# Product accumulators as one-bank PSUM tiles from pools closed and reopened inside one plan, in an attention and channel-mix kernel

## The chip, the cores and the metric

The kernel runs on one core of a Trainium2 chip. The metric is the device time of one execution in microseconds (us), from three runs. The profile comes from one further execution of the same program.

## What is computed

Sigmoid attention over 8 batches of 12 heads (448 tokens, head size 64), then a channel mix with two weight products and a gate. All is float32 to the outside.

```python
scores = q @ k.T / sqrt(64) - log(448)
attn   = sigmoid(scores) @ v                 # heads side by side: x is (8, 448, 768)
x_prev = x shifted by one token
xk, xr = mu_k * x + (1 - mu_k) * x_prev, mu_r * x + (1 - mu_r) * x_prev
k      = relu(xk @ w_k)                      # 768 -> 1024
r      = sigmoid(xr @ w_r)                   # 768 -> 768
out    = r * ((k * k) @ w_v)                 # 1024 -> 768
```

## The kernel before

**Engines.** PE does matmuls, ACT and DVE copy, cast, add and apply functions, SP issues every DMA. Each engine runs its own instructions strictly in the order in which they were recorded, and waits at each for what that one needs.

**Attention.** Two heads at a time (24 pairs), PE makes scores (L337, L346) into a PSUM tile `sc`, ACT applies the sigmoid from it (L361), PE weighs the values (L368, L376) into `av`, and `gather` (L386 to L390) reads `av` and stores xr and xk to DRAM. PSUM has eight banks: the ring `sc` is three tiles of two banks each, the ring `av` two tiles of one bank.

**Products.** Then come three stages: R (r), K (k) and V (out). Tokens are taken in four pairs of 448-token tiles; a 2x2 block product is made with seven multiplications p, in the order 0, 1, 5, 4, 6, 2, 3. One such multiplication is called a step here. A step has three rows of outputs (four in K), and `multiply` makes one row as one accumulation in one bank, L565: 9 matmuls (12 in V), since each operand is split into a high and a low part (cast by ACT, L501; remainder by DVE, L502) and three of the four partial products are made. The operands' buffers are a ring of eight (`rr0` to `rr5`, `qh`/`ql` twice).

Each row i has two accumulators. `xb[i]` takes steps 0 and 1, then 4, then 2; `yb[i]` gets a copy of `xb[i]` after step 0 (L601, ACT), then takes 5, 6 and 3. In the kernel before these are halves of the attention's tiles: `xb` is `sc0` first half, `sc0` second half, `sc1` first half, `av0`; `yb` is `sc1` second half, `sc2` first half, `sc2` second half, `av1`. So each row has banks of its own, but two banks of one `sc` tile belong to different rows. After other steps `evacuate` and `finish` read an accumulator out: with ACT (L581, L587, L605, L607) or with DVE (L609, L612, L595). `prime` (L552) writes each `yb` bank once with one matmul before the products.

**What sets the order.** Every operation is recorded in a `Plan` with an engine, a cost, a due time and keys that it reads and writes; keys are per bank (`("sc", i, h)`). The plan plays this through with its own costs and then emits the instructions in the order of their starts. The semaphores are put in behind that, by the framework that the tiles come from, from each tile's earlier writers and readers in the order of emission. The plan's keys don't reach it.

Of the kernel before, what the change touches and what calls it, by code (L numbers as in the profile page):

```python
# [8 lines left out]
F32 = mybir.dt.float32  # L9
F32R = mybir.dt.float32r  # L10
AF = mybir.ActivationFunctionType
ALU = mybir.AluOpType
U32 = mybir.dt.uint32
PSUM = bass.MemoryType.PSUM
# [8 lines left out]
class Plan:  # L23
# [8 lines left out]
    def op(self, engine, cost, prio, run, reads, writes, dma=None):  # L32
        i = len(self.ops)
        deps = set()
        for r in reads:
            if r in self.writer:
                deps.add(self.writer[r])
        for w in writes:
            if w in self.writer:
                deps.add(self.writer[w])  # L40
            deps.update(self.readers.get(w, ()))
        for r in reads:
            self.readers.setdefault(r, []).append(i)
        for w in writes:
            self.writer[w] = i
            self.readers[w] = []
        deps.discard(i)
        self.ops.append(Op(engine, cost, prio, run, deps, dma))
# [50 lines left out]
def attention_then_channel_mix(  # L99
# [15 lines left out]
    nc = tc.nc  # L115
    P = 128
    N, _, S = q.shape
# [5 lines left out]
    T = S  # L123
# [5 lines left out]
    NJH, NFH = NJ // 2, NF // 2  # L129
# [30 lines left out]
    def ring(pool, name, bufs, shape, dtype):  # L160
        return [pool.tile(shape, dtype, name=f"{name}{i}") for i in range(bufs)]

    def gap(pool, name, size):
        pool.tile([P, size // 4], F32, name=name)

    base = ctx.enter_context(tc.tile_pool(name="base", bufs=1, side="left"))
    apool = ctx.enter_context(tc.tile_pool(name="apool", bufs=1, side="right"))
    psum = ctx.enter_context(tc.tile_pool(name="psum", bufs=1, space=PSUM))

    slots = ring(base, "slot", 7, [P, 2 * WO], F32R)  # L170
    gap(base, "gap0", 64)
# [20 lines left out]
    mk = ring(apool, "mk", 2, [P, S], F32)  # L192
    mr = ring(apool, "mr", 2, [P, S], F32)
    gap(apool, "gap4", 128)
    sc = ring(psum, "sc", 3, [P, 2, 512], F32)
    av = ring(psum, "av", 2, [P, 512], F32)

    plan = Plan()
    op = plan.op
    SP, PE, ACT, DVE = "SP", "PE", "ACT", "DVE"  # L200
    SWITCH = 92

    def mm(n, cols=S):
        return n * max(cols / 2.4 + 2.5, 200)

    def act(n, sbuf=False, ptr=False):
        return 100 + 0.834 * n + 42 * sbuf + 93 * ptr

    def dve(n, fast=False, ptr=False):
        return 135 + n / (1.92 if fast else 0.96) + 61 * ptr  # L210
# [7 lines left out]
    def dma(dst, src, prio, reads, writes):  # L218
        ns = dst.shape[0] * math.prod(dst.shape[1:]) * 4 / 300
        op(SP, 500, prio, lambda: nc.sync.dma_start(dst, src), reads, writes, dma=ns)  # L220
# [94 lines left out]
    half = [slice(h * D, (h + 1) * D) for h in range(2)]  # L315
# [104 lines left out]
    for n in range(0, N, 2):  # L420
        at = n + 1
# [5 lines left out]
        at = n + 2  # L427
# [30 lines left out]
    e = N % RAW  # L458
# [12 lines left out]
    def take(n):  # L471
        return [late.pop() for _ in range(n)]

    cc, u2, rt_, p4 = take(3), take(4), take(3), take(4)
    ys += take(5 * NFH - len(ys))
    banks = [(sc[i][:, h, :T], ("sc", i, h)) for i in range(3) for h in range(2)]
    spare_banks = [(b[:, :T], ("av", i)) for i, b in enumerate(av)]
    xb, yb = banks[:3] + spare_banks[:1], banks[3:] + spare_banks[1:]

    SOURCE = {R_: xr_d, K_: xk_d, V_: k2_d}  # L480
    PAIRS = [(2 * s, 2 * s + 1) for s in range(NT // 2)]
# [1 line left out]
    def tokens(tile_):  # L483
        return slice(tile_ * T, (tile_ + 1) * T)
# [11 lines left out]
    def operand(stage, s, p, role, t, at):  # L496
        y, Y = y_of(stage, role, t)
        hi, lo, H, L = rr[nr[0] % len(rr)]
        nr[0] += 1
        used.setdefault((stage, s, p), []).append((hi, lo, H, L))  # L500
        op(ACT, act(T, True), at, lambda: nc.scalar.copy(hi, y), [Y], [H])  # L501
        op(DVE, dve(T), at, lambda: nc.vector.tensor_sub(lo, y, hi), [Y, H], [L])  # L502


    def right(stage, s, p, at):
        for t in range(KT[stage]):
# [16 lines left out]
            elif p == 3:  # L523
                minus(stage, 2, 1, 2, t, at)
                operand(stage, s, p, 2, t, at)

    hold.append(("x", R_, NJ - 1, B - 2))
    right(R_, 0, 0, N - 4)
    OFF = N + 2
# [17 lines left out]
    def slot_keys(g):  # L547
        return [("slot", g, h) + x for h in range(3) for x in ((), ("lo",))]

    def prime(i, at):  # L550
        hi, _, H, _ = used[R_, 0, 0][0]
        op(PE, mm(1, T), at, lambda: nc.tensor.matmul(yb[i][0], slots[0][:, :P], hi, start=True, stop=True, skip_group_check=True), [H] + slot_keys(0), [yb[i][1]])  # L552

    def multiply(stage, s, p, i, at):
        g = POS[p]
        bank, K = (yb if p in (5, 6, 3) else xb)[i]
        rs_ = used[stage, s, p]
        w = CW[stage]

        def go():  # L560
            n = len(rs_)
            for t, (rh, rl, _, _) in enumerate(rs_):
                hi, lo = (slots[g][:, a * n * w + t * w + i * P:a * n * w + t * w + (i + 1) * P] for a in range(2))
                for e, (a, b) in enumerate(((hi, rh), (hi, rl), (lo, rh))):
                    nc.tensor.matmul(bank, a, b, start=p in (0, 4) and (t, e) == (0, 0), stop=(t, e) == (n - 1, 2), skip_group_check=True)  # L565

        op(PE, mm(3 * len(rs_), T), at, go, [k for r in rs_ for k in r[2:]] + slot_keys(g), [K])


    def finish(stage, s, half, par, i, src, R, c, at):  # L570
        if c is None:
            u = ncc[0] % len(cc)
            ncc[0] += 1
            c, C = cc[u]
        else:
            C = R[0]
        rows = KT[R_] if stage != K_ else NFH
        m, tile_ = half * rows + i, PAIRS[s][par]
        cols = tokens(tile_)
        if stage == R_:  # L580
            op(ACT, act(T, src is c), at, lambda: nc.scalar.activation(c, src, AF.Sigmoid), R, [C])  # L581
            dma(r_d[m][:, cols], c, at, [C], [("r", m, tile_)])
        elif stage == K_:
            if src is c and half == 0:
                op(DVE, dve(T), at, lambda: nc.vector.scalar_tensor_tensor(c, src, 0.0, src, ALU.max, ALU.mult), R, [C])  # L585
            else:
                op(ACT, act(T, src is c), at, lambda: nc.scalar.activation(c, src, AF.Relu), R, [C])  # L587
                op(ACT, act(T, True), at, lambda: nc.scalar.activation(c, c, AF.Square), [C], [C])
            dma(k2_d[m][:, cols], c, at, [C], [("x", V_, m, tile_)])
        else:  # L590
            v_ = nrt[0] % len(rt_)
            nrt[0] += 1
            r, G = rt_[v_]
            dma(r, r_d[m][:, cols], at - 1.5, [("r", m, tile_)], [G])
            op(DVE, dve(T), at, lambda: nc.vector.tensor_mul(c, src, r), R + [G], [C])  # L595
            dma(out[m * P:(m + 1) * P, cols], c, at, [C], [])

    def evacuate(stage, s, p, i, at):
        (x, X), (y, Y), (u, U), (f, F) = (z[i] for z in (xb, yb, u2, p4))
        if p == 0:  # L600
            op(ACT, act(T), at, lambda: nc.scalar.copy(y, x), [X], [Y])  # L601
        elif p == 1:
            finish(stage, s, 0, 0, i, x, [X], None, at)
        elif p == 5:
            op(ACT, act(T), at, lambda: nc.scalar.copy(u, y), [Y], [U])  # L605
        elif p == 4:
            op(ACT, act(T), at, lambda: nc.scalar.copy(f, x), [X], [F])  # L607
        elif p == 6:
            op(DVE, dve(T), at, lambda: nc.vector.tensor_add(f, y, f), [Y, F], [F])  # L609
            finish(stage, s, 1, 1, i, f, [F], f, at)  # L610
        elif p == 2:
            op(DVE, dve(T), at, lambda: nc.vector.tensor_add(u, x, u), [X, U], [U])  # L612
            finish(stage, s, 0, 1, i, u, [U], u, at)
        elif p == 3:
            finish(stage, s, 1, 0, i, y, [Y], None, at)

# [4 lines left out]
    for stage, w, out7, pace in ((K_, w_k, wk_o, WK_PACE), (V_, w_v, wv_o, WV_PACE)):  # L621
        at = OFF + first[stage - 1]
        for t in range(WK_EARLY * (stage == K_), KT[stage]):
            convert_seven(w, t, KT[stage], CW[stage], pace, at, to_dram(out7, t, CW[stage]))
            at += 4 * pace
    for i in range(4):
        prime(i, OFF - 0.1 if i < NJH else OFF + 6)
    for step, (stage, s, p) in enumerate(steps):
        at = OFF + step
        if (stage, s, p) not in used:  # L630
            right(stage, s, p, at + PREP)
        rows = NFH if stage == K_ else NJH
        for i in range(rows):
            multiply(stage, s, p, i, at + i / rows)
            evacuate(stage, s, p, i, at + i / rows + EVAC)
        if stage < V_ and last[stage, p] == step:
            load_weight(stage + 1, p, OFF + max(step + 1.5, first[stage + 1] - 8 + POS[p]))
# [42 lines left out]
```

## Time and profile before

| | |
|---|---|
| three runs | 834.77, 835.23, 835.48 us, median 835.23 |
| the profiled execution | 834.95 us, of which the span of its instructions is 833.2 |
| attention on PE | about 4 to 259 us |
| stage R / K / V on PE | from about 259, 415 and 624 us |
| DMA | 179.69 MB, 216 GB/s over the span |

In rows of the timeline and of the chain the first number is the start in us from the span's start, the second the time to the end of the group, then the engine, the line, the operation, output<-inputs and the count. "[0.66 <-ACT sc L601]" means that the engine had been idle for 0.66 us just before, until that ACT instruction ended. PEld is the weight load of PE, SPq the queue of SP. A matmul of 448 columns is shown from its start to its modelled end, and the next one starts before that end.

### The profile page before, as it was taken

The numbers are of one execution on the slowest core, as the hardware profiler recorded it, in microseconds if no ns is written. First come the engines' busy times: TensorE is split into PE (matmuls) and PEld (weight loads), VectorE is DVE, ScalarE is ACT, GpSimd is POOL, SyncE is SP. The second block draws the span as 40 slices with busy tenths as digits, with TensorE's granted clock in tenths as the row PEclk, the third lists the DMA queues.
The fourth block names the chain that finished last, engine by engine and source line by source line (L and its number), as shares of the span: only waits on it lengthen the run. The fifth ranks groups of instructions, "written<-read, shape, count | busy, mean of one in ns | idle before, by whom it ended". The sixth has DMA issues, their size and how long they took to land.

```text
span 833.2 us, 13460 instructions
## 1 busy us (share of the span) xinstructions
PE 815.4 (98%) x4594; PEld 644.8 (77%) x4594; DVE 615.9 (74%) x1160; ACT 486.9 (58%) x857; POOL 0.3 (0%) x6
## 2 busy tenths in 40 slices
PE   8999999999999999999999999999999999999998
PEld 4444444544446989898989899898988989989897
DVE  3888888888898898888997727347487585776754
ACT  6787877777765545556676555555864434334341
POOL 0000000000000000000000000000000000000000
PEclk9999999999999999999999999999999999999999
DMA  7878788799986968576887542523674647555425
GB/s 230 258 258 258 241 260 264 250 300 302 318 282 230 336 223 283 190 249 228 304 263 260 165 142 112 155 89 125 222 226 143 188 155 233 158 185 175 134 67 165
DMA packets 104756, 179.69 MB, mean 216 GB/s; under 512 B 11888, under 2 KB 93296, under 8 KB 104688
## 3 DMA queue, kind: packets, MB, share of 16 engines
q1 hardware_dynamic: 104688, 178.83, 65.7%
q8 instruction: 36, 0.59, 0.3%
q14 instruction: 32, 0.26, 0.1%
HBM read 109.06 MB, written 69.73 MB: 215 GB/s over the span
## 4 chain that ended last, share of the span: by engine, by line
PE 96%; DVE 2%; ACT 1%; issue 1%; DMA 0%; DVEq 0%; SPq 0%; ACTq 0%
PE sc L565 60%; PE av L368 14%; PE sc L337 12%; PE av L565 5%; PE av L376 3%; PE sc L346 2%; ACT sc L601 1%; DVE pf L585 1%; DVE pf L612 1%; DMA qn<-in_q 0%; DVE rr L502 0%; ACT pt L587 0%; DVE slot L545 0%; ACT slot L544 0%; PE sc L552 0%
## 5 line engine op out<-in xcount | busy, mean ns | idle before, releaser
L565 PE MATMUL sc<-rr,slot 128*128 128x448 f32 x1890 | 402.8, 363 | 8.0 <-ACT sc L601 6.3
L565 PEld LDWEIGHTS sc<-rr,slot 128*128 128x128 f32 x1890 | 353.2, 187 | 36.7 <-ACT sc L601 10.0
L361 ACT ACTIVATE pf<-sc 128x896 f32<-128x896 f32 x144 | 122.7, 933 | 41.1 <-PE sc L337 41.1
L565 PE MATMUL sc<-qh,slot 128*128 128x448 f32 x420 | 138.2, 363 | 1.7 <-ACT sc L601 1.3
L368 PE MATMUL av<-pf,vn 128*64 128x448 f32 x576 | 118.6, 547 | 0.0
L565 PEld LDWEIGHTS sc<-qh,slot 128*128 128x128 f32 x420 | 78.7, 187 | 7.7 <-ACT sc L601 2.0
L368 PEld LDWEIGHTS av<-pf,vn 128*64 128x64 f32 x576 | 37.1, 136 | 59.4 <-issue 53.7
L565 PE MATMUL sc<-ql,slot 128*128 128x448 f32 x210 | 76.0, 362 | 0.0
L501 ACT CAST rr<-ys 128x448 fp32r<-128x448 f32 x66 | 36.3, 566 | 41.0 <-PE sc L565 31.8
L337 PE MATMUL sc<-qh,kh 64*128 64x448 f32 x282 | 56.8, 399 | 0.0
L337 PEld LDWEIGHTS sc<-qh,kh 64*128 64x128 f32 x282 | 26.3, 183 | 36.5 <-ACT xx L386 15.5
L337 PE MATMUL sc<-ql,kh 64*128 64x448 f32 x282 | 51.5, 362 | 0.0
L337 PE MATMUL sc<-qh,kl 64*128 64x448 f32 x282 | 51.1, 359 | 0.0
L502 DVE TENSOR_TENSOR rr<-ys,rr 128x448 fp32r<-128x448 f32 x66 | 39.0, 618 | 14.9 <-ACT rr L501 14.8
L605 ACT COPY pf<-sc 128x448 f32<-128x448 f32 x36 | 18.9, 532 | 42.1 <-PE sc L565 32.1
L313 DVE TENSOR_TENSOR kl<-kn,kh 128x384 fp32r<-128x384 f32 x47 | 26.0, 554 | 21.7 <-ACT kh L213 21.6
L565 PE MATMUL av<-rr,slot 128*128 128x448 f32 x186 | 41.8, 362 | 0.0
L565 PEld LDWEIGHTS sc<-ql,slot 128*128 128x128 f32 x210 | 39.4, 188 | 2.9
L609 DVE TENSOR_TENSOR pf<-sc,pf 128x448 f32<-128x448 f32 x24 | 15.0, 624 | 35.4 <-PE sc L565 25.8
L502 DVE TENSOR_TENSOR rr<-pf,rr 128x448 fp32r<-128x448 f32 x38 | 22.7, 620 | 24.5 <-ACT rr L501 24.4
L387 DVE TENSOR_TENSOR dx<-xx 128x448 f32<-128x448 f32 x48 | 29.9, 622 | 12.5 <-ACT xx L386 12.3
L502 DVE TENSOR_TENSOR rr<-vn,rr 128x448 fp32r<-128x448 f32 x50 | 29.6, 619 | 12.2 <-ACT rr L501 12.2
(113 smaller groups left out, 1062.4 us busy)
## 6 DMA issues: line engine op xcount, KB each, us to landing
kn<-in_k SPq DMA_DIRECT2D x48, 224.0 KB, 4.8
qn<-in_q SPq DMA_DIRECT2D x48, 224.0 KB, 5.2
vn<-in_v SPq DMA_DIRECT2D x48, 224.0 KB, 3.0
xr_d<-mr SPq DMA_DIRECT2D x48, 224.0 KB, 5.5
xk_d<-mk SPq DMA_DIRECT2D x48, 224.0 KB, 5.3
pf<-r_d SPq DMA_DIRECT2D x48, 224.0 KB, 3.3
k_d<-pf SPq DMA_DIRECT2D x34, 224.0 KB, 2.0
r_d<-pf SPq DMA_DIRECT2D x28, 224.0 KB, 2.4
```

Of the source, the lines that this page charges most:

```text
L313: op(DVE, dve(w), at, lambda src=src, hi=hi, lo=lo: nc.vector.tensor_sub(lo[i], src, hi[i]), R + [(a + "h", i)], [(a + "l", i)])
L337: nc.tensor.matmul(sc[u][:, h, :S], kk[half[h], c * P:(c + 1) * P], qq[half[h], :], start=e == 0, stop=e == len(pairs) - 1)
L346: nc.tensor.matmul(sc[u][half[h ^ (m % 2)], m % 2, :S], kn[m % RAW][half[h], KW:], qn[m % RAW][half[h], :], start=True, stop=True)
L361: op(ACT, 923, at, lambda: nc.scalar.activation(f, sc[u][:, :, :S], AF.Sigmoid, bias=NEG_LOG_S, scale=SCALE), R, K)
L368: nc.tensor.matmul(av[n % 2][half[h], :S], vn[n % 5][:, h * NC + c, :], pf[i][:, h, :], start=c == 0, stop=False)
L376: nc.tensor.matmul(av[m % 2][half[r ^ (m % 2)], :S], vn[m % 5][half[r], 2 * NC, :], pt[n // 2 % PTB][half[r], m % 2, :], start=False, stop ...
L387: op(DVE, dve(S), at, lambda: nc.vector.tensor_sub(d, x[:, 1:], x[:, :S]), [X], [G])
L501: op(ACT, act(T, True), at, lambda: nc.scalar.copy(hi, y), [Y], [H])
L502: op(DVE, dve(T), at, lambda: nc.vector.tensor_sub(lo, y, hi), [Y, H], [L])
L565: nc.tensor.matmul(bank, a, b, start=p in (0, 4) and (t, e) == (0, 0), stop=(t, e) == (n - 1, 2), skip_group_check=True)
L605: op(ACT, act(T), at, lambda: nc.scalar.copy(u, y), [Y], [U])
L609: op(DVE, dve(T), at, lambda: nc.vector.tensor_add(f, y, f), [Y, F], [F])
```

## The change

The banks of the products become eight tiles of one bank each. The attention's PSUM tiles come from two pools now, `pav` and `pscore`, and two new plan operations close a pool and open another in its place while the plan is emitted: `pscore` becomes `pb` (`xb[:3]` and `yb[:3]`) before the first product, and `pav` becomes `pb4` (`xb[3]` and `yb[3]`, used in K alone) at step 3 of all steps. Such an operation runs on no engine; its keys order it behind the last readers of the old tiles and ahead of the first writers of the new ones. As tiles exist only from then on, the products look theirs up when they are emitted (`b[0]`, `src()`, `x()`, `y()`). The fourth `prime` moves with the second pool: its due time was six steps after the first product (`OFF + 6`), and is five after it (`at + 2` at step 3). The banks are as many as before, and the operations are the same.

```diff
-    psum = ctx.enter_context(tc.tile_pool(name="psum", bufs=1, space=PSUM))
+    psa, psc = ExitStack(), ExitStack()
+    pav = psa.enter_context(tc.tile_pool(name="pav", bufs=1, space=PSUM))
+    pscore = psc.enter_context(tc.tile_pool(name="pscore", bufs=1, space=PSUM, side="right"))
...
-    sc = ring(psum, "sc", 3, [P, 2, 512], F32)
-    av = ring(psum, "av", 2, [P, 512], F32)
+    sc = ring(pscore, "sc", 3, [P, 2, 512], F32)
+    av = ring(pav, "av", 2, [P, 512], F32)
...
-    banks = [(sc[i][:, h, :T], ("sc", i, h)) for i in range(3) for h in range(2)]
-    spare_banks = [(b[:, :T], ("av", i)) for i, b in enumerate(av)]
-    xb, yb = banks[:3] + spare_banks[:1], banks[3:] + spare_banks[1:]
+    xb, yb = ([[None, (a, i)] for i in range(4)] for a in ("xb", "yb"))
+
+
+    def reopen(old, name, side, banks, after):
+        def go():
+            old.close()
+            pool = ctx.enter_context(tc.tile_pool(name=name, bufs=1, space=PSUM, side=side))
+            for i, b in enumerate(banks):
+                b[0] = pool.tile([P, 512], F32, name=f"{name}{i}")[:, :T]
+
+        op("-", 0, 0, go, [], after + [b[1] for b in banks])
...
+    reopen(psc, "pb", "right", xb[:3] + yb[:3], [("sc", u, h) for u in range(3) for h in range(2)])
     hold.append(("x", R_, NJ - 1, B - 2))
...
-                for e, (a, b) in enumerate(((hi, rh), (hi, rl), (lo, rh))):
-                    nc.tensor.matmul(bank, a, b, start=p in (0, 4) and (t, e) == (0, 0), stop=(t, e) == (n - 1, 2), skip_group_check=True)
+                for e, (l, r) in enumerate(((hi, rh), (hi, rl), (lo, rh))):
+                    nc.tensor.matmul(b[0], l, r, start=p in (0, 4) and (t, e) == (0, 0), stop=(t, e) == (n - 1, 2), skip_group_check=True)
...
-            op(ACT, act(T), at, lambda: nc.scalar.copy(y, x), [X], [Y])
+            op(ACT, act(T), at, lambda: nc.scalar.copy(y(), x()), [X], [Y])
...
-    for i in range(4):
-        prime(i, OFF - 0.1 if i < NJH else OFF + 6)
+    for i in range(3):
+        prime(i, OFF - 0.1)
     for step, (stage, s, p) in enumerate(steps):
...
+        if step == 3:
+            reopen(psa, "pb4", "left", xb[3:] + yb[3:], [("av", i) for i in range(2)])
+            prime(3, at + 2)
```

In the order of instructions, names carry the tile's number, the line numbers of the change are up to 16 higher (L565 is L576, L601 is L614, L552 is L563, L501 and L502 are L511 and L512), and brackets name the semaphores that an instruction waits for: Activation_49 is ACT's, PE_49 PE's own count, DVE_49 DVE's.

First place, PE in step 0 of the first pair: the second row of outputs, the third row, and the first matmul of step 1. Before:

```order
L565 MATMUL sc0_184<-rr0_122,slot0_114 128x448 x3
L565 MATMUL sc0_184<-rr1_123,slot0_114 128x448 x3
L565 MATMUL sc0_184<-rr2_124,slot0_114 128x448 x3
L565 MATMUL sc1_185<-rr0_122,slot0_114 128x448 [waits Activation_49]
L565 MATMUL sc1_185<-rr0_122,slot0_114 128x448 x2
L565 MATMUL sc1_185<-rr1_123,slot0_114 128x448 x3
L565 MATMUL sc1_185<-rr2_124,slot0_114 128x448 x3
L565 MATMUL sc0_184<-rr3_125,slot1_115 128x448 [waits Activation_49]
```

The same stretch after the change:

```order
L576 MATMUL pb1_2526<-rr0_125,slot0_117 128x448 x3
L576 MATMUL pb1_2526<-rr1_126,slot0_117 128x448 x3
L576 MATMUL pb1_2526<-rr2_127,slot0_117 128x448 x3
L576 MATMUL pb2_2527<-rr0_125,slot0_117 128x448 x3
L576 MATMUL pb2_2527<-rr1_126,slot0_117 128x448 x3
L576 MATMUL pb2_2527<-rr2_127,slot0_117 128x448 x3
L576 MATMUL pb0_2525<-rr3_128,slot1_118 128x448 [waits Activation_49]
```

The third row of step 0 waited for ACT at its first matmul and waits for nothing now; the first row of step 1 waits in both.

Second place, ACT from the copies of step 0 on. Before:

```order
L601 COPY sc1_185<-sc0_184 128x448 [waits PE_49,Activation_49]
L501 CAST qh0_155<-kn1_142 128x448 [waits DVE_49]
L601 COPY sc2_186<-sc0_184 128x448 [waits Activation_49]
L501 CAST qh1_156<-qn1_152 128x448 [waits DVE_49]
L601 COPY sc2_186<-sc1_185 128x448 [waits PE_49,Activation_49]
L501 CAST rr1_123<-ys0_128 128x448
```

After:

```order
L614 COPY pb3_2528<-pb0_2525 128x448 [waits PE_49,Activation_49]
L511 CAST qh0_158<-kn1_145 128x448 [waits DVE_49]
L614 COPY pb4_2529<-pb1_2526 128x448 [waits PE_49]
L511 CAST qh1_159<-qn1_155 128x448 [waits DVE_49]
L614 COPY pb5_2530<-pb2_2527 128x448 [waits PE_49]
L511 CAST rr0_125<-vn3_151 128x448 [waits DVE_49]
```

Before, one wait for PE stood ahead of the first two copies, and each copy has a wait for PE of its own now; the cast of the third operand of step 5 (`rr0<-vn`) has moved up, to right behind the copies.

Third place, PE around the fourth prime. Before, it stood behind step 1 (slot1), and the first row of step 4 (slot3) came ahead of step 5 (slot2):

```order
L565 MATMUL sc1_185<-rr5_127,slot1_115 128x448 x3
L552 MATMUL av1_188<-rr0_122,slot0_114 128x448
L565 MATMUL sc0_184<-rr1_123,slot3_117 128x448 [waits Activation_49]
L565 MATMUL sc0_184<-rr1_123,slot3_117 128x448 [waits DVE_49]
L565 MATMUL sc0_184<-rr1_123,slot3_117 128x448
```

After, it stands between step 6 (slot4) and step 2 (slot5):

```order
L576 MATMUL pb5_2530<-qh0_158,slot4_121 128x448
L563 MATMUL pb41_2565<-rr0_125,slot0_117 128x448 [waits PE_49]
L576 MATMUL pb0_2525<-qh1_159,slot5_122 128x448 [waits Activation_49]
L576 MATMUL pb0_2525<-ql1_161,slot5_122 128x448 [waits DVE_49]
L576 MATMUL pb0_2525<-qh1_159,slot5_122 128x448
L576 MATMUL pb0_2525<-rr0_125,slot5_122 128x448 [waits Activation_49]
L576 MATMUL pb0_2525<-rr0_125,slot5_122 128x448 [waits DVE_49]
```

The prime reads the buffer `rr0`, and step 2's second operand lies in `rr0` too: its cast on ACT, `L511 CAST rr0_125<-pf1_169`, has a wait for PE, since the prime has to have read the buffer, and the fourth and fifth matmul behind the prime wait for that cast and for the remainder that DVE makes of it.

More of the change, by code (lines that the diff above doesn't have):

```diff
@@ L555, in multiply @@
         g = POS[p]
-        bank, K = (yb if p in (5, 6, 3) else xb)[i]
+        b = (yb if p in (5, 6, 3) else xb)[i]
         rs_ = used[stage, s, p]
@@ L563, in go @@
                 hi, lo = (slots[g][:, a * n * w + t * w + i * P:a * n * w + t * w + (i + 1) * P] for a in range(2))
-                for e, (a, b) in enumerate(((hi, rh), (hi, rl), (lo, rh))):
-                    nc.tensor.matmul(bank, a, b, start=p in (0, 4) and (t, e) == (0, 0), stop=(t, e) == (n - 1, 2), skip_group_check=True)
-        op(PE, mm(3 * len(rs_), T), at, go, [k for r in rs_ for k in r[2:]] + slot_keys(g), [K])
+                for e, (l, r) in enumerate(((hi, rh), (hi, rl), (lo, rh))):
+                    nc.tensor.matmul(b[0], l, r, start=p in (0, 4) and (t, e) == (0, 0), stop=(t, e) == (n - 1, 2), skip_group_check=True)
+        op(PE, mm(3 * len(rs_), T), at, go, [k for r in rs_ for k in r[2:]] + slot_keys(g), [b[1]])
     def finish(stage, s, half, par, i, src, R, c, at):
-        if c is None:
+        in_sbuf = c is not None
+        if not in_sbuf:
             u = ncc[0] % len(cc)
@@ L580, in finish @@
         if stage == R_:
-            op(ACT, act(T, src is c), at, lambda: nc.scalar.activation(c, src, AF.Sigmoid), R, [C])
+            op(ACT, act(T, in_sbuf), at, lambda: nc.scalar.activation(c, src(), AF.Sigmoid), R, [C])
             dma(r_d[m][:, cols], c, at, [C], [("r", m, tile_)])
         elif stage == K_:
-            if src is c and half == 0:
-                op(DVE, dve(T), at, lambda: nc.vector.scalar_tensor_tensor(c, src, 0.0, src, ALU.max, ALU.mult), R, [C])
+            if in_sbuf and half == 0:
+                op(DVE, dve(T), at, lambda: nc.vector.scalar_tensor_tensor(c, src(), 0.0, src(), ALU.max, ALU.mult), R, [C])
             else:
-                op(ACT, act(T, src is c), at, lambda: nc.scalar.activation(c, src, AF.Relu), R, [C])
+                op(ACT, act(T, in_sbuf), at, lambda: nc.scalar.activation(c, src(), AF.Relu), R, [C])
                 op(ACT, act(T, True), at, lambda: nc.scalar.activation(c, c, AF.Square), [C], [C])
@@ L594, in finish @@
             dma(r, r_d[m][:, cols], at - 1.5, [("r", m, tile_)], [G])
-            op(DVE, dve(T), at, lambda: nc.vector.tensor_mul(c, src, r), R + [G], [C])
+            op(DVE, dve(T), at, lambda: nc.vector.tensor_mul(c, src(), r), R + [G], [C])
             dma(out[m * P:(m + 1) * P, cols], c, at, [C], [])
     def evacuate(stage, s, p, i, at):
-        (x, X), (y, Y), (u, U), (f, F) = (z[i] for z in (xb, yb, u2, p4))
+        (_, X), (_, Y), (u, U), (f, F) = (z[i] for z in (xb, yb, u2, p4))
+        x, y = (lambda: xb[i][0]), (lambda: yb[i][0])
         if p == 0:
-            op(ACT, act(T), at, lambda: nc.scalar.copy(y, x), [X], [Y])
+            op(ACT, act(T), at, lambda: nc.scalar.copy(y(), x()), [X], [Y])
         elif p == 1:
@@ L604, in evacuate @@
         elif p == 5:
-            op(ACT, act(T), at, lambda: nc.scalar.copy(u, y), [Y], [U])
+            op(ACT, act(T), at, lambda: nc.scalar.copy(u, y()), [Y], [U])
         elif p == 4:
-            op(ACT, act(T), at, lambda: nc.scalar.copy(f, x), [X], [F])
+            op(ACT, act(T), at, lambda: nc.scalar.copy(f, x()), [X], [F])
         elif p == 6:
-            op(DVE, dve(T), at, lambda: nc.vector.tensor_add(f, y, f), [Y, F], [F])
-            finish(stage, s, 1, 1, i, f, [F], f, at)
+            op(DVE, dve(T), at, lambda: nc.vector.tensor_add(f, y(), f), [Y, F], [F])
+            finish(stage, s, 1, 1, i, lambda: f, [F], f, at)
         elif p == 2:
-            op(DVE, dve(T), at, lambda: nc.vector.tensor_add(u, x, u), [X, U], [U])
-            finish(stage, s, 0, 1, i, u, [U], u, at)
+            op(DVE, dve(T), at, lambda: nc.vector.tensor_add(u, x(), u), [X, U], [U])
+            finish(stage, s, 0, 1, i, lambda: u, [U], u, at)
         elif p == 3:
```

## Prediction

> **What bounds the kernel now.** The page comes first: which engine is full, at which clock. Then the waits of PE, since it is the one.
>
> ```profile
> span 833.2 us, 13460 instructions
> PE 815.4 (98%) x4594; PEld 644.8 (77%) x4594; DVE 615.9 (74%) x1160; ACT 486.9 (58%) x857; POOL 0.3 (0%) x6
> PEclk9999999999999999999999999999999999999999
> ...
> PE sc L565 <- ACT sc L601: 7.6, 12, 0.7
> PE sc L337 <- DMA qn<-in_q: 4.0, 1, 4.0
> PE sc L565 <- DVE pf L612: 2.0, 4, 0.7
> PE sc L565 <- ACT pf L587: 0.2, 1, 0.2
> ```
>
> PE sets the time, at the full clock from end to end. It waits for four things only. One is the first load (4.0 us), which the change doesn't touch. The others are in the products: 12 waits for the copy L601 (one for each of 4 pairs in 3 stages), 4 for L612, 1 for L587. No wait for an operand (L501, L502) is in the list.
>
> Next, the timeline of PE and of ACT at the first such wait.
>
> ```profile
> 258.28 0.98 PE L376 MATMUL av<-pt,vn 64*64 64x448 f32 x8
> 259.20 0.88 PE L552 MATMUL sc<-rr,slot 128*128 128x448 f32 x3
> 259.91 3.76 PE L565 MATMUL sc<-rr,slot 128*128 128x448 f32 x18
> 264.33 7.48 PE L565 MATMUL sc<-rr,slot 128*128 128x448 f32 x36 [0.66 <-ACT sc L601]
> 271.65 0.36 PE L552 MATMUL av<-rr,slot 128*128 128x448 f32 x1
> ...
> 292.25 7.36 PE L565 MATMUL sc<-rr,slot 128*128 128x448 f32 x36
> ...
> 828.70 0.37 PE L565 MATMUL sc<-qh,slot 128*128 128x448 f32 x1
> ```
>
> ```profile
> 259.34 0.97 ACT L386 COPY xx<-av 128x448 f32<-128x448 f32 x2 [1.39 <-issue]
> 263.76 0.52 ACT L601 COPY sc<-sc 128x448 f32<-128x448 f32 x1 [3.45 <-PE sc L565]
> ```
>
> A matmul is shown 0.36 us long, but 36 of them without a wait take 7.36, so one starts every (7.36 - 0.36) / 35 = 0.200 us. Step 0's first row is therefore done by about 259.91 + 9 x 0.2 + 0.16 = 261.9. ACT is free from 260.31, yet copies that row at 263.76 only, 0.09 behind the end of the *second* row (259.91 + 3.76 = 263.67). And the third row starts at 264.33, 0.05 behind the copy's end (264.28), though the copy doesn't touch its bank. Two false waits follow each other: the copy reads `sc0`'s first half and waits for the second half's row, which had been emitted ahead of it; the third row goes into `sc1`'s first half and waits for the copy, which writes `sc1`'s second half. Both pairs share a tile, and no bank. The order of PE and ACT shown in the section on the change says the same: that wait of PE is gone, and each copy has its own wait for PE.
>
> **What a wait costs.** By the idle time in the list the three kinds come to 7.6 + 2.0 + 0.2 = 9.8 us. By the starts they cost more. The third row would have started at 259.91 + 18 x 0.2 = 263.51 and started at 264.33, 0.82 late; and the 36 matmuls behind it took 7.48 in place of 7.36, another 0.12. The idle time leaves out the 0.16 us by which the last matmul ahead of a wait is shown beyond the next start, and the slow restart. The chain of waits gives it by pair, since the stretch behind each copy is one row there:
>
> ```profile
> 303.28 38.10 PE sc L565 x189
> 342.03 38.09 PE sc L565 x189
> ...
> 471.91 2.08 PE sc L565 x9
> ...
> 523.85 2.08 PE sc L565 x9
> ...
> 680.61 50.69 PE sc L565 x252
> 731.90 50.69 PE sc L565 x252
> ```
>
> From one copy to the next, R: 342.03 - 303.28 = 38.75, less 189 x 0.2 = 37.80, is 0.95. V: 51.29 less 252 x 0.2 = 50.40 is 0.89. K: 51.94 less 50.40 is 1.54, of which 0.89 for the copy as in V and 0.65 for L612. In sum 4 x 0.95 + 8 x 0.89 + 4 x 0.65, and 0.3 more for the one long wait for L612 (0.7 us in the list, the other three (2.0 - 0.7) / 3 = 0.43), and 0.2 + 0.16 + 0.12 = 0.5 for L587: **14.3 us**. Check over the whole: the products are 4 pairs x 7 steps x (27 + 36 + 36) = 2772 matmuls and 4 primes, from 259.20 to the last start at 828.70. That is 569.50, less 2775 x 0.2 = 555.0, makes 14.5; the last 0.2 is the first prime and rounding. I take 14.3, not 9.8, because the starts are counted and the ends modelled; with 9.8 the sum below would end 4.5 higher, at 825.7. The Trainium skill, page "Perfetto Trace Analysis", section "Identifying the Most-Contended Engine", says that matmul busy time is a bad measure of the room left, as matmuls are pipelined; the trace agrees (9.8 idle against 14.3 lost).
>
> **The change part by part.**
>
> *One-bank tiles.* All three kinds of wait are between banks of one tile: L601 as above; L612 and L587 read row three from `sc1`'s first half while the next step's first row wants `sc1`'s second half. With a tile per bank they go: -14.3. What is late next? The same accumulator's own reader: step 1's first row waits for the copy of its own bank, which now starts as its row ends and has two more rows, 2 x 1.8 = 3.6 us, for 0.09 + 0.52. Operands have never been waited for, and their ring is freed by PE itself, so they follow PE: PE gains 0.9 us per pair against them, not the sum. Only in the first pair does the order move: step 5 comes whole right behind step 1, at about 259.2 + 0.7 + 54 x 0.2 = 270.7. In before its third operand was ready late:
>
> ```profile
> 272.05 0.57 ACT L501 CAST rr<-vn 128x448 fp32r<-128x448 f32 x1 [0.57 <-PE av L552]
> ...
> 272.65 0.63 DVE L502 TENSOR_TENSOR rr<-vn,rr 128x448 fp32r<-128x448 f32 x1
> ...
> 276.41 0.69 DVE L234 SCALAR_TENSOR_TENSOR wbits<-wraw,wbits 128x512 uint32<-128x512 uint32 x1
> ```
>
> That was because `rr0` was held for the fourth prime at 271.65. Now the cast stands behind the third copy, at about 266, and the remainder is there by 268: no cost. If it stayed at 273.28, step 5's eighth matmul (due at 272.1) would wait 1.2 once, which rival 1 covers.
>
> *Reopened pools.* They run on no engine. `pb` needs the last sigmoid of `sc`; `pb4` needs `gather`'s copies of `av`, ended at 260.31 (above), some 25 us ahead of its prime.
>
> ```profile
> 254.81 1.76 ACT L361 ACTIVATE pf<-sc 128x896 f32<-128x896 f32 x2
> ```
>
> It ended at 256.57, and PE weighs values until 259.26 anyway: no cost. The two primes with a wait for PE's own count have no such row in before. If it meant the matmul just ahead, 0.36 to land in place of the next start at 0.2, with a restart of 0.12, it is 0.3 each; a gain is excluded, as a wait starts nothing sooner. I take 0: the scores wrote `sc` last, ahead of all the weighing, and `av` is done 25 us before its prime.
>
> *The fourth prime* has moved ahead of step 2, and there it has a price. From its start the same chain is in before: prime 271.65, cast 272.05 to 272.62, remainder 272.65 to 273.28, 1.63 us. Step 2's fifth matmul wants that remainder and would start 5 x 0.2 = 1.0 behind the prime: 1.63 + 0.05 - 1.0 = 0.68 late, with the restart 0.12: **+0.8**, once. Ends: 0 if the buffer were free earlier, 1.5 if DVE, which has weight conversions queued ahead (0.69 us each, the last row above), comes late. Behind that cast ACT has the next operands, which PE wants 5 us later; the fetch into `pf1` on SP waits for that remainder too, and with it SP's whole queue, in before at this place:
>
> ```profile
> 281.64 2.09 SPq L220 DMA_DIRECT2D pf<-xr_d  x3
> ...
> 291.36 1.56 SPq L220 DMA_DIRECT2D pf<-wk_o  x2
> ```
>
> That fetch now goes out near 289 (the prime at 270.7 + 81 x 0.2 = 286.9, and the chain of 1.7) and feeds step 5 of the second pair at about 309: no cost.
>
> *The end.* Rows two and three of the last step are halves of `sc2`.
>
> ```profile
> 829.10 1.16 DVE L595 TENSOR_TENSOR pt<-sc,pf 128x448 f32<-128x448 f32 x2 [2.98 <-PE sc L565]
> 829.75 0.86 SPq L220 DMA_DIRECT2D out<-pt  x2
> ```
>
> Both multiplications wait for the last matmul. Now row two's runs while PE works on row three, and one is left behind the end: -(1.16 - 0.62) = **-0.5**. Ends: 0 and 1.0, if the last store also lands faster without the other beside it.
>
> **The sum:** -14.3 + 0.8 - 0.5 = -14.0. The profiled execution would go from 834.95 to 820.95 (span 833.2 to 819.2). It lies 0.28 below the median of the runs, so the median goes from 835.23 to **821.2**.
>
> **Rivals.**
> 1. *Part of it.* PE now runs into operands or conversions. In R, DVE is fullest:
>
> ```profile
> 259.10:412.60 153.50, 150.85 (x752) 139.96 (x749) 133.32 (x256) 85.10 (x172) 0.00 (x0) 1.00 0.74 252
> ```
>
> 133.32 of 153.50 us there, 89% of the 149.7 left without R's waits: not a bound by sum, but conversions stand ahead of operands in its fixed order. For it: the order in the first pair was made by the plan's own costs. Against: no operand was waited for in before. If a fifth to two thirds of the gain goes, 824 to 831.
> 2. *It doesn't do what it says.* A gap that repeats 12 times could also come from too few banks, and they stay eight, with the same roles; the waits would come back under another name: 835.2. The Trainium skill, "Perfetto Trace Analysis", section "Optimization Strategy", gives that reading of consistent bubbles. Against it: the third row's bank had no reader at 263.51, and the order shows the wait gone.
> 3. *Slower: DVE's queue becomes the bound in R.* If each of R's 28 steps waited for one conversion of 0.69 us ahead of its operand, that is 19.3 us: 821.2 + 19.3 = 840.5. It turns the sign from 14.0 / 28 = 0.5 us per step. For it: DVE is busy for 87% of that stage. Against: a conversion's due time is that of no operand, and PE never waited for L502.
>
> **Chances.** Forecast (within 1.5 us of 821.2, by the ends of prime, store and reopened pools): 0.75. Rival 1: 0.18, rival 2: 0.04, rival 3: 0.03. The range reaches from 819.8 (no price for the prime, 1.0 at the end, and some rounding) to 826.0, which takes in the sum by idle time and the near part of rival 1. A measurement of this kernel can tell about 0.2% (1.7 us) from no change; by that, faster 0.93, same 0.04, slower 0.03.
>
> **What would show it.** In the profile after: no wait of PE for L614 (the copies), L625 (L612) or L599 (L587); copies that start 0.1 behind the end of their own row; stretches of 189 and 252 matmuls in 37.8 and 50.4 us from pair to pair; one wait of PE near 287 for a cast and remainder of `rr<-pf`, under 1 us in all; one multiplication behind the last matmul. Wrong it would be if waits for L511 or L512 appear in later steps (rival 1 or 3), or waits for another reader of the accumulators at the old places (rival 2).

## The result, and the profile after

| | before | after |
|---|---|---|
| median of the runs | 835.00 us (834.67 to 835.48, 4 runs) | 820.87 us (820.23 to 821.55, 4 runs) |
| the profiled execution, and its span | 834.95, 833.2 | 820.23, 818.4 |
| first product matmul's start (the first prime) | 259.20 | 258.68 |
| last product matmul's start | 828.70 | 814.59 |
| from there to the end of the span | 4.50 | 3.81 |

The ratio is 0.983, with a 95% interval from 0.9813 to 0.9847. Predicted were 821.2 us, between 819.8 and 826.0.

The page of after, and the waits of PE:

```profile
span 818.4 us, 13513 instructions
PE 810.7 (99%) x4594; PEld 646.0 (79%) x4594; DVE 620.1 (76%) x1160; ACT 498.1 (61%) x857; POOL 0.3 (0%) x6
...
PE sc L339 <- DMA qn<-in_q: 4.0, 1, 4.0
PE pb L576 <- DVE rr L512: 0.2, 1, 0.2
```

DVE and ACT are as busy as they were to within 2.5%, and PE is shown busy for 4.7 us less than before although it does the same matmuls. About 0.5 of that is a difference in attention, which the next section shows to be chance; the rest had been waits hidden in the busy time, since the last matmul ahead of a wait is shown 0.16 us beyond the next start and those behind it took 0.12 us longer, by the rows of before in the prediction. All waits for accumulators are gone from the list. One wait is new, for the remainder that L512 makes.

The timeline of PE in after, at the first pair, at the fourth prime, and at the end:

```profile
258.68 0.88 PE L563 MATMUL pb<-rr,slot 128*128 128x448 f32 x3
259.39 10.96 PE L576 MATMUL pb<-rr,slot 128*128 128x448 f32 x54
...
286.39 0.36 PE L563 MATMUL pb<-rr,slot 128*128 128x448 f32 x1
...
287.41 0.47 PE L576 MATMUL pb<-rr,slot 128*128 128x448 f32 x1
288.07 1.28 PE L576 MATMUL pb<-rr,slot 128*128 128x448 f32 x5 [0.19 <-DVE rr L512]
289.19 0.36 PE L576 MATMUL pb<-qh,slot 128*128 128x448 f32 x1
...
814.59 0.36 PE L576 MATMUL pb<-qh,slot 128*128 128x448 f32 x1
```

Steps 0 and 1 of the first pair are now one run of 54 matmuls: (10.96 - 0.36) / 53 = 0.200 us from start to start, with no hole where the third row had waited. Around the prime the tenth matmul behind it should start 2.0 later, at 288.39, and starts at 289.19: 0.80 late. The fourth matmul, at 287.41 in place of 287.19, is late for the cast; the fifth, at 288.07 in place of 287.39, for the remainder. The chain that ended last has the products in two long pieces, one up to the prime and one from this fifth matmul to the end:

```profile
259.55 27.00 PE pb L576 x135
288.07 526.89 PE pb L576 x2633
```

(526.89 - 0.36) / 2632 is again 0.200: not one further hole in 2633 matmuls.

The timeline of ACT in after, at the copies of step 0:

```profile
261.45 0.52 ACT L614 COPY pb<-pb 128x448 f32<-128x448 f32 x1 [1.65 <-PE pb L576]
261.88 0.57 ACT L511 CAST qh<-kn 128x448 fp32r<-128x448 f32 x1
263.19 0.52 ACT L614 COPY pb<-pb 128x448 f32<-128x448 f32 x1 [0.74 <-PE pb L576]
...
264.99 0.52 ACT L614 COPY pb<-pb 128x448 f32<-128x448 f32 x1 [0.80 <-PE pb L576]
265.42 0.57 ACT L511 CAST rr<-vn 128x448 fp32r<-128x448 f32 x1
```

The first row's last matmul ends at 259.39 + 8 x 0.2 + 0.36 = 261.35, and its copy starts at 261.45, 0.10 behind the end of its *own* row; in before it stood 0.09 behind the end of the second row. The three copies are 1.8 apart, as the rows are.

The time that went, from the starts: the products take 814.59 - 258.68 = 555.91 us in place of 569.50, 13.6 less; the end takes 0.7 less; and attention came to its end 0.5 earlier, which the next section shows to be chance. 13.6 + 0.7 + 0.5 = 14.8, which is the difference of the spans; without the chance it is 14.3, and the medians differ by 14.1.

### The profile page after: what moved, and what is told of

It is laid out like the page before. It is cut to its first block, busy times and chain, and to the rows that moved or that the text cites. A ratio compares the mean times of both kernels' runs of the same rounds, so it can differ in the third digit from the quotient of the medians.

```text
span 818.4 us, 13513 instructions
## 1 busy us (share of the span) xinstructions
PE 810.7 (99%) x4594; PEld 646.0 (79%) x4594; DVE 620.1 (76%) x1160; ACT 498.1 (61%) x857; POOL 0.3 (0%) x6
## 4 chain that ended last, share of the span: by engine, by line
PE 99%; DMA 0%; DVE 0%; ACT 0%; SPq 0%; issue 0%
PE pb L576 68%; PE av L370 14%; PE sc L339 12%; PE av L378 3%; PE sc L348 2%; DMA qn<-in_q 0%; PE pb L563 0%; DVE rr L512 0%; DVE pt L607 0%; ACT rr L511 0%; SPq L222 0%
## 5 line engine op out<-in xcount | busy, mean ns | idle before, releaser
L576 PE MATMUL pb<-rr,slot 128*128 128x448 f32 x2076 | 437.4, 362 | 0.2 <-DVE rr L512 0.2
L576 PEld LDWEIGHTS pb<-rr,slot 128*128 128x128 f32 x2076 | 389.1, 187 | 26.9 <-DVE rr L512 0.5
L576 PE MATMUL pb<-qh,slot 128*128 128x448 f32 x464 | 151.8, 361 | 0.0
L576 PEld LDWEIGHTS pb<-qh,slot 128*128 128x128 f32 x464 | 87.0, 187 | 6.4
L576 PE MATMUL pb<-ql,slot 128*128 128x448 f32 x232 | 84.2, 363 | 0.0
L511 ACT CAST rr<-ys 128x448 fp32r<-128x448 f32 x66 | 36.4, 566 | 45.9 <-PE pb L576 45.1
L512 DVE TENSOR_TENSOR rr<-ys,rr 128x448 fp32r<-128x448 f32 x66 | 39.2, 619 | 11.6 <-ACT rr L511 11.6
L576 PEld LDWEIGHTS pb<-ql,slot 128*128 128x128 f32 x232 | 43.5, 188 | 2.3
L512 DVE TENSOR_TENSOR rr<-pf,rr 128x448 fp32r<-128x448 f32 x38 | 23.2, 623 | 26.4 <-ACT rr L511 26.4
L614 ACT COPY pb<-pb 128x448 f32<-128x448 f32 x40 | 20.7, 518 | 33.6 <-PE pb L576 33.6
L618 ACT COPY pf<-pb 128x448 f32<-128x448 f32 x40 | 21.3, 532 | 31.4 <-PE pb L576 27.0
L511 ACT CAST rr<-vn 128x448 fp32r<-128x448 f32 x50 | 27.9, 565 | 18.9 <-PE pb L576 17.6
L512 DVE TENSOR_TENSOR rr<-vn,rr 128x448 fp32r<-128x448 f32 x50 | 29.7, 621 | 10.5 <-ACT rr L511 10.4
```

The source lines that it names most:

```text
L576: nc.tensor.matmul(b[0], l, r, start=p in (0, 4) and (t, e) == (0, 0), stop=(t, e) == (n - 1, 2), skip_group_check=True)
L614: op(ACT, act(T), at, lambda: nc.scalar.copy(y(), x()), [X], [Y])
L618: op(ACT, act(T), at, lambda: nc.scalar.copy(u, y()), [Y], [U])
```

## The experiments

The theory: an instruction waits for the latest earlier user of a whole *tile*, and two rows whose banks are in one tile wait for each other though their banks differ. Rivals: the gain comes from something else that the change does (pools of their own and their reopening, or the order that the plan makes with them); or every shared tile costs its share by itself. For each kernel the comparison is by the median, and by the length of the products from the first start to the last, which no chance in attention touches (569.50 before, 555.91 after). In kernels that group banks, two lines were added, so L576 is L578, L614 is L616, L512 is L514, L622 is L624 and L625 is L627 there; L565 is the prime there (L563 in after), and L601 the Relu (L587 in before, L599 in after).

### The changed kernel once more

> The changed kernel once more, as the measure for the other three of this set, since they differ from it by less than two medians of different sets can tell. Every theory expects 820.9 us again (between 820.2 and 821.6, as in its four runs). Beside it stands a question: in the first profile the first product matmul came 0.5 us earlier than in the profile of the kernel before (258.68 against 259.20), though attention wasn't changed. If that is chance of one execution, this profile may show either value; if pools of their own do it, it shows 258.7 again.

820.92 us (820.66 to 821.4; the kernel before beside it 834.92; ratio 0.9831, 0.9818 to 0.9845). The products take 555.90. The first product matmul starts at 259.23 this time, 0.03 from where it did in before; the end, 819.0 - 815.13 = 3.87, is 0.63 shorter than in before. So the 0.5 was chance. It arises in the first twelve matmuls of attention, as the chain of each shows; in later profiles they took up to 4.85. First before, then after, then the repeat:

```profile
3.97 4.62 PE sc L337 x12
```

```profile
3.95 4.14 PE sc L339 x12
```

```profile
4.15 4.49 PE sc L339 x12
```

### The fourth prime on another operand

```diff
-    def prime(i, at):
-        hi, _, H, _ = used[R_, 0, 0][0]
+    def prime(i, at, p=0):
+        hi, _, H, _ = used[R_, 0, p][0]
...
-            prime(3, at + 2)
+            prime(3, at, 4)
```

> The changed kernel with the fourth prime on an operand of step 4, due at step 4's start, so that rr0 is no longer held for it until step 2. Theory (the prime's place costs 0.8 us, the one stall of PE left in the products): no wait of PE between the first product matmul and the last, and 0.8 us less than the changed kernel, 820.1. Rival (the time goes elsewhere, since ACT and DVE now have that cast and remainder earlier and something else comes late): a wait under another name and 820.9.

820.25 us (819.82 to 820.88; ratio 0.9822, 0.9809 to 0.9835). The products take 815.24 - 260.13 = 555.11, 0.80 less than after's, and this is all that PE waits for:

```profile
PE sc L339 <- DMA qn<-in_q: 4.0, 1, 4.0
```

The term of 0.8 is shown by the profile to the second digit. By the medians it is 0.7, and the intervals of the two ratios overlap, so the runs alone would not tell these kernels apart.

### The old pool, with the halves of a tile given to one row

```diff
-    xb, yb = banks[:3] + spare_banks[:1], banks[3:] + spare_banks[1:]
+    xb, yb = banks[0::2] + spare_banks[:1], banks[1::2] + spare_banks[1:]
```

This is the kernel before with that one line changed.

> The kernel before, with its one PSUM pool and its tiles of two banks, and one line changed: each sc tile's two halves are the two accumulators of one row (xb[i], yb[i]), no longer of two rows. Theory (all waits come from two rows in one tile, and the size of a tile, the number of pools and their reopening have no price): no PE wait for the copies of step 0, for the Relu or for the additions into u2; one multiplication behind the last matmul; the fourth prime stands behind step 1 as in the kernel before and costs nothing. 835.0 - 14.3 - 0.5 = 820.2 us, 0.7 below the changed kernel. Rival (a two-bank tile is itself what couples the copy and the matmul, or reopened pools bring the gain): 12 waits for the copy stay, 835 us; if waits for the second bank of the own row come in their place, between 822 and 835.

820.39 us (819.85 to 820.93; ratio 0.9824, 0.9811 to 0.9838). PE's list of waits is the first load alone:

```profile
PE sc L337 <- DMA qn<-in_q: 4.0, 1, 4.0
```

The products take 815.25 - 260.14 = 555.11, and the end 3.85. Tiles of two banks, one pool and the old lookups give all that the change gives, without the stall at the prime. Neither the size of a tile nor the reopening is what counts, but whose banks share a tile.

### The reopened pools, with the old pairs

```diff
-            for i, b in enumerate(banks):
-                b[0] = pool.tile([P, 512], F32, name=f"{name}{i}")[:, :T]
+            for i, g in enumerate(banks):
+                t = pool.tile([P, len(g), 512], F32, name=f"{name}{i}")
+                for h, b in enumerate(g):
+                    b[0] = t[:, h, :T]
...
-    reopen(psc, "pb", "right", xb[:3] + yb[:3], ...)
+    reopen(psc, "pb", "right", [xb[:2], [xb[2], yb[0]], yb[1:3]], ...)
```

> The changed kernel with pools closed and reopened as it does, and its order in the plan, but the six banks of pb as three tiles of two banks in the pairs of the kernel before (xb[0] with xb[1], xb[2] with yb[0], yb[1] with yb[2]). Theory: everything that was gained is lost again, 14.3 for the waits and 0.5 at the end, so 820.9 + 14.8 = 835.7 us, with 12 PE waits for the copy of step 0, and 0.8 of it is the fourth prime's stall, which stays. Rival (reopened pools, or the order that the plan made with them, bring a part of the gain): less than 834, down to 821 if they bring all of it.

838.70 us (837.62 to 838.89; ratio 1.004, 1.0027 to 1.0053): slower than before, and 3.0 above what was expected. The waits of PE:

```profile
PE pb L578 <- ACT pb L616: 7.6, 12, 0.7
PE sc L339 <- DMA qn<-in_q: 4.0, 1, 4.0
PE pb L578 <- DVE pf L627: 2.0, 4, 0.7
PE pb L578 <- ACT rr L513: 1.4, 1, 1.4
PE pb L578 <- DVE rr L514: 0.3, 1, 0.3
```

The waits in the first and third line are those of the kernel before to the digit. The last two are the fourth prime's: the stall that should be 0.8 is larger. The timeline of PE there, then ACT's, then DVE's:

```profile
288.39 0.36 PE L578 MATMUL pb<-qh,slot 128*128 128x448 f32 x1
288.59 0.36 PE L565 MATMUL pb<-rr,slot 128*128 128x448 f32 x1
...
292.85 0.36 PE L578 MATMUL pb<-qh,slot 128*128 128x448 f32 x1
```

```profile
289.45 0.58 ACT L595 ACTIVATE pf<-pf 128x448 f32<-128x448 f32 x1 [2.31 <-DVE pf L624]
289.93 0.55 ACT L513 CAST rr<-vn 128x448 fp32r<-128x448 f32 x1
290.39 0.56 ACT L513 CAST rr<-pf 128x448 fp32r<-128x448 f32 x1
```

```profile
288.79 0.62 DVE L624 TENSOR_TENSOR pf<-pb,pf 128x448 f32<-128x448 f32 x1 [1.34 <-PE pb L578]
```

The tenth matmul behind the prime starts 4.26 later in place of 2.0, so the stall is 2.26. Read it backwards: the cast into `rr0` stands in ACT's queue behind a sigmoid, which waits for DVE's addition of step 6's second row. That addition starts at 288.79, 0.04 behind the end of the third row's last matmul (288.39 + 0.36), though its own row had been done nine matmuls, 1.8 us, before. It is the same false wait, now from the pair `yb[1]`, `yb[2]`, which in the kernel before reached only the end: there the prime stood elsewhere, and PE waited for nothing behind that addition. A run below, with the prime moved away, tests this.

### Each old pair by itself

The groups were `[xb[:2], ...]`, `[[xb[2], yb[0]], ...]`, both, and `[yb[1:3], ...]`, with all other accumulators in tiles of one bank.

> The changed kernel with one of the old pairs alone: xb[0] and xb[1] as the halves of one tile, all other accumulators in tiles of one bank. Theory (each of the 12 waits is a chain of two false waits, and needs both pairs): the copy of step 0's first row starts late, 0.1 behind the end of the second row, but nothing waits for it, as it writes yb[0], which has a tile of its own; the copies still end 1.2 ahead of step 1. No PE wait for the copy, 820.9 us like the changed kernel. Rival (each shared tile costs its share, as a wait is paid wherever two rows share a tile): of the 14.3 us a half to a third comes back, 825 to 828.

> The changed kernel with the other old pair alone: xb[2] and yb[0] in one tile. Theory: the third row of step 0 has to wait for the copy into yb[0], but this copy now starts at the end of the first row and is done 0.6 later, while the second row still runs: no PE wait for it. What comes back are the waits for L612 (row three of step 2 read from the tile into which step 3's first row goes) in K, 4 x 0.65 + 0.3, and perhaps the 0.5 for the Relu: 820.9 + 2.9 = 823.8 us, up to 824.3. Rival (each shared tile costs its share): half or more of the 14.3 comes back, with waits for the copy, 828 to 832.

> The changed kernel with both of these pairs (xb[0] with xb[1], xb[2] with yb[0]), and yb[1] and yb[2] in tiles of their own. Theory (a chain of two): the 12 waits for the copy are back, and the waits for L612: +14.3, so 835.2 us (834.7 without the wait for the Relu), with a stall of 0.8 at the fourth prime and a stretch of 3.9 from the last matmul's start to the end, as in the changed kernel. It is 3 below the 838.7 with all three pairs. Rival (shares add up): the sum of what the two pairs cost alone.

> The changed kernel with the third old pair alone: yb[1] and yb[2] in one tile. With all three pairs, 838.7 us came out where 835.7 was expected, and its trace shows the addition L612 of step 6's second row 1.8 us late (it waits for the third row, in the same tile), ACT's queue behind it, and the cast into rr0 behind that: PE's stall at the fourth prime grew from 0.8 to 2.3. Theory: this comes from this pair alone, so the stall of 2.3 is here too (+1.5), and both last multiplications wait for the last matmul (+0.6): 820.9 + 2.1 = 823.0 us. Rival (the longer stall comes from the PE waits elsewhere, which shift ACT's queue): a stall of 0.8, and only the end is longer: 821.5.

Products and end are in us, as in the first table, each from one profile.

| pairs in one tile | median (range) | ratio to before, 95% | products | the end |
|---|---|---|---|---|
| xb0 with xb1 | 821.02 (820.89 to 821.60) | 0.9833 (0.9819 to 0.9848) | 555.95 | 3.86 |
| xb2 with yb0 | 820.42 (820.08 to 821.05) | 0.9825 (0.9809 to 0.9842) | 555.94 | 3.87 |
| both of these | 835.02 (834.24 to 835.69) | 0.9999 (0.9990 to 1.0008) | 570.00 | 3.83 |
| yb1 with yb2 | 823.19 (822.76 to 824.44) | 0.9860 (0.9846 to 0.9875) | 557.37 | 4.50 |

Two pairs that cost nothing alone cost 14.1 together: alone, each leaves the products within 0.04 us of after's 555.91; together they make them 570.00. That settles the chain of two, and the rival of shares falls. The timelines show how either half comes to nothing. Here is the copy of step 0's first row on ACT, and then steps 0 and 1 on PE, with `xb[0]` and `xb[1]` in one tile:

```profile
263.85 0.52 ACT L616 COPY pb<-pb 128x448 f32<-128x448 f32 x1 [3.45 <-PE pb L578]
```

```profile
260.00 11.02 PE L578 MATMUL pb<-rr,slot 128*128 128x448 f32 x54
```

And the copy with `xb[2]` and `yb[0]` in one tile:

```profile
261.76 0.52 ACT L616 COPY pb<-pb 128x448 f32<-128x448 f32 x1 [1.65 <-PE pb L578]
```

With the first pair the copy is as late as in before, 0.09 behind the end of the second row (260.00 + 17 x 0.2 + 0.36 = 263.76), but PE goes through its 54 matmuls without waiting for it. With the second pair the copy is on time, 0.10 behind the end of its own row (that row starts at 259.70 there: 259.70 + 8 x 0.2 + 0.36 = 261.66), and is over before the third row is due. The waits of PE with both pairs:

```profile
PE pb L578 <- ACT pb L616: 7.6, 12, 0.7
PE sc L339 <- DMA qn<-in_q: 4.1, 1, 4.1
PE pb L578 <- DVE pf L627: 1.2, 3, 0.4
PE pb L578 <- ACT slot L557: 0.7, 1, 0.7
PE pb L578 <- DVE rr L514: 0.2, 1, 0.2
```

The fourth wait for L612 in before, the one of 0.7, is not in this list; at its place PE waits 0.7 for a cast of weights (L557).

One expectation missed: the second pair alone should have brought back the waits for L612 (L627 here), 2.9 us, and did not. The additions of step 2 on DVE in stage K show why, first in before, with the row of PE that waits for the third of them, then with that pair alone:

```profile
508.23 0.62 DVE L612 TENSOR_TENSOR pf<-sc,pf 128x448 f32<-128x448 f32 x1 [0.82 <-PE sc L565]
...
509.83 0.62 DVE L612 TENSOR_TENSOR pf<-sc,pf 128x448 f32<-128x448 f32 x1
...
511.44 0.61 DVE L612 TENSOR_TENSOR pf<-sc,pf 128x448 f32<-128x448 f32 x1
...
512.20 1.04 PE L565 MATMUL sc<-rr,slot 128*128 128x448 f32 x4 [0.41 <-DVE pf L612]
```

```profile
500.33 0.63 DVE L627 TENSOR_TENSOR pf<-pb,pf 128x448 f32<-128x448 f32 x1
...
502.13 0.63 DVE L627 TENSOR_TENSOR pf<-pb,pf 128x448 f32<-128x448 f32 x1
...
503.93 0.63 DVE L627 TENSOR_TENSOR pf<-pb,pf 128x448 f32<-128x448 f32 x1
```

With the second pair alone each addition comes with its row, 1.8 apart, and the third is over while the fourth row still runs. In before the first one waits for the second row (the pair `xb[0]`, `xb[1]`), DVE's queue fills behind it, and its additions follow 1.6 apart with other work between, all late. Only then is the third too late for the row that shares its tile. So this wait is a chain of two as well.

The fourth kernel came out as expected: 557.37 - 555.91 = 1.46 for the longer stall at the prime, and 0.6 at the end.

### The prime moved away, with the old pairs

The last two kernels with old pairs, each with the prime of the kernel of 820.25:

> The kernel with all three old pairs (838.7 us), with the fourth prime on an operand of step 4 as in the kernel of 820.25, so that no buffer is held for it. Theory (reopened pools cost nothing, all that is left over the kernel before was the stall of 2.3 at the prime): no wait for a cast or remainder of rr<-pf; the products take 571.4 - 2.3 = 569.1 us from the first start to the last, against 569.5 in the kernel before, and the time is that of the kernel before, 834.9 (834.3 to 835.9). Rival (reopened pools or the plan's other order have a price of their own, which made up part of the 838.7): 836.4, which is 838.7 less 2.3, or more.

> yb[1] and yb[2] in one tile (823.2 us), with the fourth prime on an operand of step 4. Theory (this pair acts on PE only through the buffer rr0 that the prime holds): no PE wait in the products, 555.1 us from their first start to the last, and only the end is longer by 0.6, as both last multiplications wait for the last matmul: 820.25 + 0.6 = 820.9 us. Rival (the late additions of step 6 delay other operands as well): a wait under another name, 822 or more.

With all three pairs 835.25 us (834.45 to 835.85), before beside it 835.07; ratio 1.0001, 0.9992 to 1.0009. With `yb[1]` and `yb[2]` alone, 820.89 (820.45 to 821.28), products 555.11, end 4.47. So reopened pools, the indirect lookup and the plan's order have no price that these runs can tell. In the first of the two, the products take 829.00 - 259.28 = 569.72 in place of the 569.1 expected, since a wait of 0.4 for a Relu (L587 in before) is back:

```profile
PE pb L578 <- ACT pf L601: 0.4, 1, 0.4
```

In the kernel with the first two pairs and in that of 838.70 it was PE's weight load alone that waited for this Relu, and in the kernels with one pair neither PE nor its weight load did:

```profile
PEld pb L578 <- ACT pf L601: 0.2, 1, 0.2
```

A part stays open: moving the prime took 1.7 off these products (571.43 to 569.72), but 3.4 off the median. 0.7 of the rest is attention's start in the two profiles (259.94 against 259.28). Three of the five runs of the kernel of 838.70 had a mean granted clock of 0.997 or 0.998 and took about 1 us longer than the two at 1.0 (837.62 and 837.90); the runs don't show why the clock was lower there. The two kernels were also measured on different chips; against the kernel before beside each, the difference is 3.6 us (3.78 above it, and 0.18).

### A larger dose

The kernel of 835.25 us, with the three groups made one:

```diff
-    [xb[:2], [xb[2], yb[0]], yb[1:3]]
+    [xb[:3] + yb[:3]]
```

> The six accumulators of rows 1 to 3 as one tile of six banks, with the fourth prime on an operand of step 4: the same cause in a far larger dose. Every reader of a row now waits for the row emitted ahead of it, and the row after that waits for that reader. In the order of the instructions 182 rows come to wait for a reader whose own wait is for the matmul just ahead of them (115 of ACT, 67 of DVE), against 12 in the kernel before, and 12 more are one matmul apart. Theory: each costs what one cost there, about 0.92 for a reader on ACT and 1.05 for one on DVE, whose operations take 0.1 longer: 106 + 70 + 10 = 186, so 820.3 + 0.6 + 186 = 1007 us, and up to 1060 where DVE's queue makes its readers later still. Rival (the waits were a matter of these 12 places, and elsewhere there is room between reader and row): well under 950.

1013.23 us in one run. The largest of PE's waits:

```profile
PE pb L578 <- DVE pf L627: 21.4, 29, 0.8
PE pb L578 <- ACT pb L616: 18.1, 28, 0.7
PE pb L578 <- ACT pf L620: 17.4, 28, 0.7
PE pb L578 <- DVE pf L624: 15.2, 20, 1.1
```

The whole list has 201 waits in the products, 198 for readers of accumulators and 3 for casts, and the products take 747.7 us, 192.6 more than the 555.11 without them: 0.96 each, against 0.89 to 0.95 for one wait for the copy in the kernel before. The forecast by count, 1007, is 0.6% off in the time, and its 186 us of waits 3.4% below the 192.6.

## Why the prediction was right

**What bounds it, and the price of a wait.** The sum was -14.0, and the medians differ by 14.1. Counting starts gave 14.3 for the waits, the idle time 9.8. The products became 13.6 shorter with a stall of 0.8 that is new, so 14.4 went in the profiles: the starts were right to 0.1, and the sum by idle time would have missed by 4.6. Of that loss PE's busy time had hidden nearly a third.

**Two false waits that follow each other.** The mechanism was right, and it is shown from both sides: taken away without the change's means (one line in the old kernel), brought back with all of them (the old pairs in new pools), and halved, where either half is free.

**The waits for L612 and L587.** They went, and a total of 14.4 against 14.3 leaves little room for an error in their size, which no run shows by itself. The step on L612 failed in its cause: it put them down to one tile, `sc1`, and the second pair alone had no such wait. They needed DVE's additions to be late as well, and those were held up by the first pair. The step gave `sc1` as the cause of the wait for L587 too (0.5 of the sum). The second pair alone did not bring that one back either, and with both pairs only the weight load waited for the Relu, so it too takes more than the one tile; what sets its size stays open.

**The fourth prime.** Sized as 0.8 from rows of before, measured 0.80 twice (in the profile after, and by taking it away). Its upper end of 1.5, from DVE's queue, wasn't reached here, but it is no bound for such a stall: with the pair `yb[1]`, `yb[2]` it became 2.26, and through ACT's queue.

**The end.** Forecast -0.5, measured -0.6 to -0.7. The multiplication that no longer stands behind the last matmul is the most of it, as the rows of DVE in after show, each behind its own row:

```profile
812.58 0.63 DVE L607 TENSOR_TENSOR pt<-pb,pf 128x448 f32<-128x448 f32 x1 [1.77 <-PE pb L576]
814.98 0.62 DVE L607 TENSOR_TENSOR pt<-pb,pf 128x448 f32<-128x448 f32 x1 [1.77 <-PE pb L576]
```

**Reopened pools at nothing, the first pair's order at nothing, SP's fetch at nothing.** Right. The third operand's cast of step 5 is in the rows of ACT above, at 265.42, and step 5 follows without a hole. The fetch into `pf1` went out at 288.04; the prediction's own sum gives 286.9 + 1.7 = 288.6, and the half microsecond between is the one by which attention ended earlier in this profile:

```profile
288.04 0.32 SPq L222 DMA_DIRECT2D pf<-xr_d  x1
```

**The rivals.** None came. Operands and conversions never held PE up in after outside the prime. Too few banks, the reading of repeated holes that the prediction took from the Trainium skill, is excluded: eight banks with 12 holes and eight banks without differ in one line. A rule bears on what the waits have to guard. The Trainium skill, page "PSUM — Partial Sum Buffer", section "PSUM bank collisions raise a hardware error", wants accesses to PSUM guarded by bank and group of 32 partitions, not by address; what the framework guarded here was the tile, two banks wide, and the 14.4 us are what that excess cost. The runs show only that one bank may be read while another bank, of the same tile or not, is written at no loss (products of 555.11 us with either kind of tile); collisions were no part of them.

## What to carry to other kernels

Where a semaphore follows tiles, lay out a tile so that only operations which have to wait for each other anyway share it: one row's two accumulators could, while two rows' made each other wait. Measure a repeated wait by the starts of the instructions around it and not by idle time, which here showed 9.8 of 14.4 us. And before believing that one wait is one cause, look at what made the releaser late: here two couplings cost 14.1 us together and nothing apart.

## What was not expected of the hardware

The first twenty matmuls of attention took between 5.05 us (4.14 for twelve, 0.91 for the next eight; after) and 6.44 us (4.85 and 1.59; the old pool with the halves of a tile given to one row) from one profiled execution to the next, with the same instructions. That is 1.39 of the 1.46 us between the earliest and the latest start of the products (258.68 and 260.14). Why they differ is open. It may be a part of the spread between the runs of one kernel (after: 820.23 to 821.55), but the runs without a profile have no trace, so that isn't shown.
